# Routing attention and a gated feed-forward layer on one core: cluster masks through a TensorE product, weight conversion in two VectorE operations

## The chip, the cores and the metric

The kernel runs on one core of a Trainium2 chip. A core has five engines that run side by side and meet through semaphores: TensorE (PE in the profile) multiplies matrices into PSUM, VectorE (DVE), ScalarE (ACT) and GpSimd (POOL) work element by element, and SyncE (SP) issues transfers. The metric is the device time of one execution in microseconds (us). Before the change the median of four runs is 1229.87 us (1224.88 to 1232.32).

## The reference, cut to what matters

For each of 4 batches and 8 heads there are 768 queries and keys of 64 elements. Every query and every key is assigned to the nearest of 16 centroids of its head, and a query sees only the keys of its own cluster. The attention output, 3072 rows of 512, then goes through a feed-forward layer.

```python
q_assign = np.argmax(einsum(q_n, c_n), axis=-1)      # 16 clusters
k_assign = np.argmax(einsum(k_n, c_n), axis=-1)
mask = q_assign[:, :, :, None] == k_assign[:, :, None, :]
scores = np.where(mask, scale * q @ k.T, -1e9)
attn = softmax(scores);  x = attn @ v
h = x @ w_in                                          # 512 -> 2048
g = h * erf(softplus(h))
out = g @ w_out                                       # 2048 -> 512
```

The first maximum wins where two clusters tie, as argmax has it. The two weight matrices arrive as eight-byte floats, so they have to be made into four-byte ones on the chip.

## The kernel before, in words

**Attention.** The work goes by pairs of heads: 16 pairs, four to a batch. A pair has 12 units (two halves of the queries, six tiles of 128 keys). For a unit, `products` multiplies keys by queries in f32 and `scores` adds to it, in the same PSUM tile `sc`, a bf16 product `km` by `qm`. This second product carries the mask: `qm` holds, per query, ones at its cluster (and a row with its largest masked score), and `km` holds, per key, 0 at its own cluster and a hugely negative number at the others. One exponential on ScalarE makes `pr` from `sc`, GpSimd adds up `pr` into `acc`, and `attend` multiplies by the values into `av`. `divide` makes the reciprocal of the sums and writes `xT`, the input of the feed-forward layer.

**Preparing a pair.** What a pair needs beforehand is a generator, `aside(p)`, made of `route` and `shift` and cut into steps by its yields. `route` (line 272) has six steps: transpose the queries and keys; multiply them by the centroids into `psim`; transpose this into `sims`, take the maximum `mx` of each 16 and replace `sims` by a 0/1 comparison with it; copy the keys (`vectors("k")`); multiply by `rank` (16, 15, ... for queries, the same times 2 to the 60th for keys), take the maximum `mr` again, compare (queries: equal; keys: minus), giving `hot`, and transpose this to `hotT`; lastly spread `hotT` into `qm` and `km` by two VectorE and six ScalarE operations. The rank settles ties. `shift` (line 348) has fourteen steps: 24 bf16 products `sm` with a VectorE maximum `nmx` each, and for either half a transpose `pn`, a copy `nmT` on ScalarE and six small transfers that put the maxima into `qm`.

**Converting weights.** The weights come in 32 blocks (16 of `w_in`, 16 of `w_out`), each 128 x 512 eight-byte numbers, taken apart as the high word `hi` and the low word `lo`. `convert` (line 205) makes a block in three steps: the maximum with a tiny number of the magnitude that ScalarE has put into `x`; a shift by 3 and an AND of it, with the next transfer (`fetch`) issued behind; and an OR with two bits of `hi`, after which GpSimd adds the rounding summand `m` that ScalarE has made from `lo`. `split` holds the two ScalarE operations of the next block. `prepare(n)` runs n steps.

**The order of the work.** Through the first four pairs (48 slots, one per unit) nothing else is there to do, and every engine's order is the program's up to slot 44. A table `plan` says for each of a pair's 12 slots how many steps of its own `aside`, of the next pair's `aside` (before and after the scores) and of the conversion are run. From slot 45 on the feed-forward stream of `hidden` (products `hp`, copied to `g`), `gate` (softplus, erf, a product) and `project` (products `po`) is pumped between the attention's products, and a planner orders the instructions of each engine by its own costs. In that part `ASIDE` (line 45) lists the places at which a step of the next pair's `aside` is run, and the conversion is called with `prepare(2)` until it is done. `gate` and the last blocks of `w_out` share the tiles `a_s`.

PSUM has two buffers for `sc` and four (tag "x") for everything else: `psim`, `sm`, `pn`, `av`, `psum`, `hp`, `po`.

Of the kernel before, what the change touches and what calls it, by code (L numbers as in the profile page):

```python
# [8 lines left out]
F32 = mybir.dt.float32  # L9
BF16 = mybir.dt.bfloat16  # L10
U32 = mybir.dt.uint32
I32 = mybir.dt.int32
ALU = mybir.AluOpType
ACT = mybir.ActivationFunctionType
AX = mybir.AxisListType
# [17 lines left out]
LC = 512  # L33
TINY_HI = 2.0**-15
OUT_AT = (1, 2, 3, 4, 2, 3, 4, 2, 3, 4, 4, 3, 4, 4, 4, 4)
# [8 lines left out]

ASIDE = (*range(5), 6, *range(8, 8 + 2 * NJ), 10 + 2 * NJ, 12 + 2 * NJ)
REST = 3
# [20 lines left out]
def kernel(  # L67
# [36 lines left out]
    minus = const.tile([P, D], F32, name="minus")  # L104
    rank = const.tile([P, C], F32, name="rank")
    ccT = const.tile([P, HP, 2 * C], F32, name="ccT")
# [55 lines left out]
    for t in prs:  # L162
        ge.memset(t[:, :, HW : HW + 2], EPS)

# [31 lines left out]
    def split(n):  # L198

        if n < len(w_steps):  # L200
            hi, lo, m, x = steps[n]
            ae.activation(out=x.bitcast(F32), in_=hi.bitcast(F32), func=ACT.Abs)
            ae.activation(out=m.bitcast(I32), in_=lo, func=ACT.Copy, scale=2.0**-29)

    def convert():

        split(0)
        for n in range(len(w_steps)):
            hi, _, m, x = steps[n]
            w = w_steps[n][0]  # L210
            xf = x.bitcast(F32)
            ve.tensor_scalar(out=xf, in0=xf, scalar1=TINY_HI, scalar2=None, op0=ALU.max)
            yield
            ve.tensor_scalar(
                out=x, in0=x, scalar1=3, scalar2=0x3FFFFFFF,
                op0=ALU.logical_shift_left, op1=ALU.bitwise_and,
            )

            fetch(n - 2 if n < n_w_in else n - 1)
            yield  # L220
            ve.scalar_tensor_tensor(
                out=w.bitcast(U32), in0=hi, scalar=0xC0000000, in1=x,
                op0=ALU.bitwise_and, op1=ALU.bitwise_or,
            )

            ge.tensor_tensor(out=w.bitcast(I32), in0=w.bitcast(I32), in1=m.bitcast(I32), op=ALU.add)
            converted[0] = n + 1
            split(n + 1)
            yield
# [42 lines left out]
    def route(p):  # L272
# [20 lines left out]
        def vectors(nm):  # L293
# [12 lines left out]
        mx = routep.tile([P, n], F32, name="mx")  # L306
        ve.reduce_max(out=mx, in_=sim, axis=AX.X)
        ve.tensor_tensor(
            out=sim, in0=sim, in1=mx.unsqueeze(2).to_broadcast([P, n, C]), op=ALU.is_equal
        )  # L310
        yield
        vectors("k")
        yield

        ve.tensor_tensor(
            out=sim, in0=sim, in1=rank.unsqueeze(1).to_broadcast([P, n, C]), op=ALU.mult
        )
        mr = routep.tile([P, n], F32, name="mr")
        ve.reduce_max(out=mr, in_=sim, axis=AX.X)

        hot = routep.tile([P, HW], BF16, name="hot")
        for r, op in ((slice(0, D), ALU.is_equal), (slice(D, P), ALU.subtract)):
            ve.tensor_tensor(
                out=hot[r].rearrange("p (g c) -> p g c", c=C), in0=sim[r],
                in1=mr[r].unsqueeze(2).to_broadcast([D, n, C]), op=op,
            )
        hotT = routep.tile([P, HW], BF16, name="hotT")
        ve.transpose(out=hotT, in_=hot)
        yield
        late = []  # L330
        for half in range(2):
            cols = slice(half * HW, (half + 1) * HW)
            for e in range(2):
                r = slice(e * D, e * D + Q)
                g = slice(half * Q, (half + 1) * Q)
                if half == 0:
                    ve.tensor_scalar_mul(out=low["q"][r, e, cols], in0=hotT[g], scalar1=own[g, e : e + 1])
                else:
                    late.append((low["q"][r, e, cols], hotT[g], own[g, e : e + 1]))
                g = slice(D + half * Q, D + (half + 1) * Q)  # L340
                ae.copy(out=low["k"][r, e, cols], in_=hotT[g])
        for dst, src, scale in late:
            ae.activation(out=dst, in_=src, func=ACT.Copy, scale=scale)
        yield
# [245 lines left out]
    def prepare(n):  # L590
        for _ in range(n):
            next(conv, None)
# [3 lines left out]
    def aside(p):  # L596
# [5 lines left out]
    plan = (  # L602
        (1, 0, 1, 1), (1, 0, 2, 0), (1, 0, 2, 0), (1, 0, 1, 0), (0, 0, 0, 0), (0, 0, 2, 0),
        (0, 0, 2, 1), (0, 0, 2, 1), (0, 1, 0, 3), (0, 0, 0, 3), (0, 0, 2, 1), (0, 0, 1, 2),
    )
# [3 lines left out]
    def advance(p, n):  # L609
        for _ in range(n):  # L610
            next(ready[p])
# [11 lines left out]
    ve.memset(minus, -1.0)  # L623
    for c in range(C):
        ve.memset(rank[0:D, c : c + 1], float(C - c))
    ve.tensor_scalar_mul(out=rank[D:P], in0=rank[0:D], scalar1=BIG)
    ve.memset(alleps, S * EPS)
# [10 lines left out]
    products(1)  # L638
    advance(0, 4)
    prepare(2)  # L640
# [39 lines left out]
    for u in range(2 * NJ * HP, len(units), 2):  # L680
# [12 lines left out]
        for i in range(SLOTS):  # L693
# [3 lines left out]
            if not resting[0]:  # L697
                prepare(2)
            next(part, None)
# [41 lines left out]
```

## Time and profile before

| | |
|---|---|
| median of four runs | 1229.87 us |
| the profiled execution | 1224.88 us |
| its span, first to last instruction | 1223.1 us |
| PE busy | 1155.2 us, 94% of the span |
| DVE busy | 539.3 us, 44% |
| ACT busy | 568.1 us, 46% |
| POOL busy | 465.7 us, 38% |
| ACT table loads | 113 of 1283 ns |

The page gives the busy time of each engine, then the span cut into 40 slices of about 30.6 us with the busy share of each engine in tenths, the clock granted to PE, and the transfers. Other views group the instructions by operation and tile, follow the chain of work that ended last, or sum the busy time in stretches that one chooses. In a group's row the figures are: name of output and inputs, shapes, count, total busy us, mean ns of one, then the idle time of the engine before them and what ended it. All of the kernel's operations are issued through one helper, so that their rows carry its line, L58, and the names of the tiles tell them apart.

### The profile page before, as it was taken

What the parts mean: (1) busy time and instruction counts of PE and PEld (TensorE: products, weight loads), DVE (VectorE), ACT (ScalarE), POOL (GpSimd) and SP (SyncE); (2) the same over time, 40 slices, a digit from 0 to 9 for tenths busy, and PEclk for the clock granted to TensorE, in tenths of its full rate; (3) what the DMA queues carried; (4) which work ended last, traced back from release to release, by engine and by line L of the source; (5) the groups of instructions that cost most, each with busy time, mean ns of one, the idle gap of its engine ahead of it and who ended that gap; (6) DMA issues with size and microseconds to landing.
All of it is one profiled execution on the core that took longest, in us unless ns stands there. A gap on an engine that the chain in (4) does not pass through costs nothing.

```text
span 1223.1 us, 13359 instructions
## 1 busy us (share of the span) xinstructions
PE 1155.2 (94%) x4897; PEld 618.3 (51%) x4897; DVE 539.3 (44%) x999; ACT 568.1 (46%) x675; POOL 465.7 (38%) x462
## 2 busy tenths in 40 slices
PE   4888888889999999999999999999999999999998
PEld 1222235654454445465465455556456456576663
DVE  6899885674544335443353345344435112011121
ACT  3666656658342637175364454356263264132222
POOL 2467764446333344144243334235234343030200
PEclk7899999999999999999999999999999999999999
DMA  7444323122020202020110201002000000000000
GB/s 134 81 101 108 78 83 84 53 93 40 9 48 9 48 1 40 9 35 14 25 32 1 48 10 27 22 10 39 9 22 1 9 9 1 18 1 17 1 18 18
DMA packets 140753, 42.95 MB, mean 35 GB/s; under 512 B 133520, under 2 KB 133520, under 8 KB 140688
## 3 DMA queue, kind: packets, MB, share of 16 engines
q1 hardware_dynamic: 137552, 41.70, 15.1%
q10 hardware_dynamic: 3136, 0.39, 0.3%
q8 instruction: 39, 0.64, 0.2%
q14 instruction: 26, 0.21, 0.1%
HBM read 35.68 MB, written 6.29 MB: 34 GB/s over the span
## 4 chain that ended last, share of the span: by engine, by line
PE 74%; DVE 11%; issue 7%; ACT 6%; DMA 2%; POOL 1%; SPq 0%; ACTq 0%; DVEq 0%; POOLq 0%
PE po L58 25%; PE hp L58 24%; PE sc L58 12%; PE av L58 7%; PE sm L58 4%; DVE nmx L58 3%; ACT L58 2%; DVE w_out L58 2%; DVE den L58 1%; PE psum L58 1%; ACT inv L58 1%; DVE sims L58 1%; PE psim L58 1%; ACT km L58 1%; ACT a_s L58 1%
## 5 line engine op out<-in xcount | busy, mean ns | idle before, releaser
L58 PE MATMUL hp<-xT,w_in 128*128 128x256 f32 x1536 | 385.3, 388 | 3.3 <-DVE xT L58 2.4
L58 PE MATMUL po<-w_out,g 128*128 128x512 f32 x768 | 367.8, 597 | 0.6 <-DVE den L58 0.6
L58 POOL TENSOR_TENSOR acc<-acc,pr 128x384 f32<-128x384 f32 x256 | 240.1, 967 | 312.2 <-ACT pr L58 312.0
L58 PEld LDWEIGHTS hp<-xT,w_in 128*128 128x128 f32 x1536 | 287.8, 192 | 123.0 <-issue 79.2
L58 DVE TENSOR_REDUCE nmx<-sm 128x1 f32<-128x384 f32 x384 | 195.4, 551 | 140.4 <-PE sm L58 139.6
L58 ACT ACT_TABLE_LOAD x113 | 145.0, 1283 | 230.7 <-DVE g L58 128.8
L58 ACT ACTIVATE pr<-sc 128x768 f32<-128x768 f32 x192 | 147.4, 807 | 164.3 <-PE sc L58 164.0
L58 PEld LDWEIGHTS po<-w_out,g 128*128 128x128 f32 x768 | 141.8, 190 | 107.2 <-issue 94.4
L58 PE MATMUL sc<-qT,kT 64*128 64x384 f32 x768 | 182.5, 530 | 6.3 <-ACT pr L58 6.2
L58 POOL TENSOR_TENSOR g<-a_s,g 128x512 f32<-128x512 f32 x88 | 111.1, 1293 | 200.5 <-ACT a_s L58 200.5
L58 DVE COPY g<-hp 128x512 f32<-128x512 f32 x96 | 66.0, 687 | 256.5 <-PE hp L58 256.3
L58 PE MATMUL av<-pr,in_v 128*64 128x386 f32 x768 | 143.5, 502 | 2.9 <-DVE nmx L58 2.9
L58 PE MATMUL sm<-km,qm 128*128 128x384 bf16 x384 | 105.4, 340 | 29.9 <-DVE nmx L58 13.8
L58 PEld LDWEIGHTS sc<-qT,kT 64*128 64x128 f32 x768 | 70.4, 190 | 85.5 <-issue 44.3
L58 POOL TENSOR_TENSOR acc<-pr,pr 128x384 f32<-128x384 f32 x64 | 66.2, 1056 | 93.6 <-ACT pr L58 93.6
L58 PEld LDWEIGHTS av<-pr,in_v 128*64 128x64 f32 x768 | 49.8, 137 | 91.9 <-issue 77.3
L58 PEld LDWEIGHTS <-qm 128*128 128x128 bf16 x384 | 35.2, 99 | 97.0 <-issue 70.8
L58 DVE SCALAR_TENSOR_TENSOR den<-psum,inv 128x384 f32<-128x384 f32 x32 | 17.8, 558 | 145.5 <-ACT inv L58 145.0
L58 ACT ACTIVATE a_s<-a_s 128x2048 f32<-128x2048 f32 (+2 forms) x40 | 55.9, 1414 | 16.1 <-DMA a_s<-in_moe_w_out_dram 12.4
L58 ACT ACTIVATE a_s<-g 128x2048 f32<-128x2048 f32 x24 | 45.9, 1912 | 34.4 <-DVE g L58 33.0
L58 PE MATMUL sc<-qm,km 64*128 64x384 bf16 x384 | 58.7, 325 | 2.1 <-DMA qm<-nmT 2.1
L58 ACT COPY nmT<-pn 6x128 bf16<-6x128 bf16 x32 | 8.1, 252 | 95.2 <-PE pn L58 94.8
(66 smaller groups left out, 602.5 us busy)
## 6 DMA issues: line engine op xcount, KB each, us to landing
w_out<-in_moe_w_in_dram SPq DMA_DIRECT2D x16, 512.0 KB, 4.6
in_q<-in_q_dram SPq DMA_DIRECT2D x64, 96.0 KB, 3.2
in_v<-in_v_dram SPq DMA_DIRECT2D x32, 192.0 KB, 3.0
out_dram<-osb SPq DMA_DIRECT2D x24, 256.0 KB, 2.0
in_k<-in_k_dram SPq DMA_DIRECT2D x60, 96.0 KB, 3.4
a_s<-in_moe_w_out_dram SPq DMA_DIRECT2D x8, 512.0 KB, 3.7
w_out<-in_moe_w_out_dram SPq DMA_DIRECT2D x8, 512.0 KB, 4.2
qm<-nmT SPq DMA_DIRECT2D x192, 0.2 KB, 1.7
```

The source lines that it names most:

```text
L58: ins = getattr(self.engine, name)(*args, **kw)
```

## The change

**Masks.** After the comparison with `mx`, which now writes `hot` in bf16, the transpose to `hotT` follows at once; the product with `rank`, the second maximum `mr` and the two comparisons of 64 rows are gone. Instead a constant 128 x 128 bf16 matrix `first` is made at the start by GpSimd (one fill, three selections): within each block of 16 clusters it holds 1 on the diagonal and -1 for every earlier cluster. One bf16 product of `first` and `hotT` goes into a PSUM tile `won` (tag "x"), which is 1 where a cluster is the first maximum and 0 or less elsewhere. `qm` is made of it by a product with `own` and a maximum with 0 (VectorE, two operations) and by Relu with that scale (ScalarE, two operations); `km` by Identity with scale 2 to the 60th and bias minus that (ScalarE, four operations). These eight now read PSUM. `route` has five steps instead of six.

**Conversion.** A block takes two VectorE steps. ScalarE's Abs scales by 2 to the 16th, so that the maximum with 2.0 and a shift by 3 alone give the magnitude's bits. A new ScalarE operation in `signs` (Prelu) writes the sign into the upper 16 bits of each word of the summand `m`, and GpSimd's addition puts it in. The OR with `hi` is gone. `fetch` is called after the maximum, and the plan's conversion steps per pair go from 12 to 8, four blocks a pair as before.

**Order.** `plan` and `ASIDE` are rewritten for 19 instead of 20 steps; the conversion in the later part is called with 1 and 2 steps by turns.

```diff
-        ve.tensor_tensor(
-            out=sim, in0=sim, in1=mx.unsqueeze(2).to_broadcast([P, n, C]), op=ALU.is_equal
-        )
+        hot = routep.tile([P, HW], BF16, name="hot")
+        ve.tensor_tensor(
+            out=hot.rearrange("p (g c) -> p g c", c=C), in0=sim,
+            in1=mx.unsqueeze(2).to_broadcast([P, n, C]), op=ALU.is_equal,
+        )
+        hotT = routep.tile([P, HW], BF16, name="hotT")
+        ve.transpose(out=hotT, in_=hot)
         yield
         vectors("k")
         yield
-        ve.tensor_tensor(
-            out=sim, in0=sim, in1=rank.unsqueeze(1).to_broadcast([P, n, C]), op=ALU.mult
-        )
-        mr = routep.tile([P, n], F32, name="mr")
-        ve.reduce_max(out=mr, in_=sim, axis=AX.X)
-        hot = routep.tile([P, HW], BF16, name="hot")
-        for r, op in ((slice(0, D), ALU.is_equal), (slice(D, P), ALU.subtract)):
-            ve.tensor_tensor(
-                out=hot[r].rearrange("p (g c) -> p g c", c=C), in0=sim[r],
-                in1=mr[r].unsqueeze(2).to_broadcast([D, n, C]), op=op,
-            )
-        hotT = routep.tile([P, HW], BF16, name="hotT")
-        ve.transpose(out=hotT, in_=hot)
-        yield
+        won = ps_x.tile([P, HW], F32, name="won", tag="x")
+        te.matmul(won, lhsT=first, rhs=hotT, start=True, stop=True)
...
                 if half == 0:
-                    ve.tensor_scalar_mul(out=low["q"][r, e, cols], in0=hotT[g], scalar1=own[g, e : e + 1])
+                    ve.tensor_scalar(
+                        out=low["q"][r, e, cols], in0=won[g], scalar1=own[g, e : e + 1], scalar2=0.0,
+                        op0=ALU.mult, op1=ALU.max,
+                    )
                 else:
-                    late.append((low["q"][r, e, cols], hotT[g], own[g, e : e + 1]))
+                    ae.activation(
+                        out=low["q"][r, e, cols], in_=won[g], func=ACT.Relu, scale=own[g, e : e + 1]
+                    )
                 g = slice(D + half * Q, D + (half + 1) * Q)
-                ae.copy(out=low["k"][r, e, cols], in_=hotT[g])
-        for dst, src, scale in late:
-            ae.activation(out=dst, in_=src, func=ACT.Copy, scale=scale)
+                ae.activation(
+                    out=low["k"][r, e, cols], in_=won[g], func=ACT.Identity, bias=nbig[g], scale=BIG
+                )
...
-            ae.activation(out=x.bitcast(F32), in_=hi.bitcast(F32), func=ACT.Abs)
+            ae.activation(out=x.bitcast(F32), in_=hi.bitcast(F32), func=ACT.Abs, scale=UP)
...
+    def signs(n):
+        hi, _, m, _ = steps[n]
+        ae.activation(
+            out=m.bitcast(I16)[:, 1 : 2 * LC : 2], in_=hi.bitcast(F32), func=ACT.Prelu,
+            scale=2.0**-25, alpha=2.0**90,
+        )
...
-            ve.tensor_scalar(out=xf, in0=xf, scalar1=TINY_HI, scalar2=None, op0=ALU.max)
+            ve.tensor_scalar(out=xf, in0=xf, scalar1=2.0, scalar2=None, op0=ALU.max)
+            signs(n)
+            fetch(n - 2 if n < n_w_in else n - 1)
             yield
             ve.tensor_scalar(
-                out=x, in0=x, scalar1=3, scalar2=0x3FFFFFFF,
-                op0=ALU.logical_shift_left, op1=ALU.bitwise_and,
-            )
-            fetch(n - 2 if n < n_w_in else n - 1)
-            yield
-            ve.scalar_tensor_tensor(
-                out=w.bitcast(U32), in0=hi, scalar=0xC0000000, in1=x,
-                op0=ALU.bitwise_and, op1=ALU.bitwise_or,
+                out=w.bitcast(U32), in0=x, scalar1=3, scalar2=None, op0=ALU.logical_shift_left
             )
...
     plan = (
-        (1, 0, 1, 1), (1, 0, 2, 0), (1, 0, 2, 0), (1, 0, 1, 0), (0, 0, 0, 0), (0, 0, 2, 0),
-        (0, 0, 2, 1), (0, 0, 2, 1), (0, 1, 0, 3), (0, 0, 0, 3), (0, 0, 2, 1), (0, 0, 1, 2),
+        (1, 0, 1, 0), (1, 0, 2, 0), (1, 0, 1, 0), (1, 0, 0, 0), (0, 0, 1, 1), (0, 0, 1, 1),
+        (0, 0, 2, 1), (0, 0, 2, 1), (0, 1, 0, 2), (0, 1, 0, 0), (0, 0, 2, 1), (0, 0, 1, 1),
     )
...
-    advance(0, 4)
+    advance(0, 3)
...
-                prepare(2)
+                prepare(1 + i % 2)
```

## The prediction

> **What bounds the kernel now.** I read the page's line of 40 slices first, because an average over the span hides the stages.
>
> ```profile
> PE   4888888889999999999999999999999999999998
> DVE  6899885674544335443353345344435112011121
> PEclk7899999999999999999999999999999999999999
> ```
>
> From the tenth slice on (about 275 us) PE is full and VectorE half idle: there the time is PE's work. In the first nine PE is not full and VectorE nearly is. The change is about VectorE, so I cut that part by pairs of heads, each beginning with the transpose of its queries, and set the later part beside it (columns: busy us with counts for PE, weight loads, DVE, ACT, POOL; then the granted clock, the transfers' share and GB/s):
>
> ```profile
> 32.25:69.00 36.75, 31.18 (x152) 9.85 (x153) 30.51 (x57) 23.97 (x37) 20.03 (x20) 0.91 0.44 104
> 69.00:106.00 37.00, 31.63 (x166) 10.05 (x166) 33.85 (x61) 23.16 (x36) 25.55 (x25) 1.00 0.39 90
> 106.00:142.50 36.50, 31.19 (x156) 9.70 (x156) 31.79 (x59) 22.85 (x37) 24.06 (x24) 0.95 0.38 90
> 142.50:180.00 37.50, 28.99 (x143) 10.59 (x142) 33.01 (x54) 21.60 (x35) 28.26 (x25) 0.95 0.35 83
> 180.00:300.00 120.00, 109.05 (x493) 67.56 (x492) 74.88 (x129) 78.46 (x90) 65.12 (x57) 0.96 0.26 67
> 500.00:1223.00 723.00, 716.14 (x2921) 409.27 (x2919) 226.02 (x409) 290.35 (x306) 219.85 (x214) 1.00 0.07 17
> ```
>
> In the four pair periods VectorE has 31 to 34 of some 37 us, PE is idle for 5.57, 5.37, 5.31 and 8.51 us (24.8 together), and ScalarE has 13 to 16 us free per period. From 180 to 300 us PE is idle for another 11.0 us; after 500 us for 6.9 of 723. What can be won lies before 300 us.
>
> Then the chain that ended last, between 100 and 148 us (start, length, work): does it pass through the operations that go?
>
> ```profile
> 107.75 0.80 DVE w_out L58
> ...
> 112.74 1.10 DVE sims L58
> ...
> 113.86 0.56 DVE mr L58
> ...
> 114.45 0.55 DVE hot L58
> ...
> 115.01 0.57 DVE hot L58
> ...
> 134.98 0.69 DVE w_in L58
> ```
>
> It does: the product with the rank (1.10), the second maximum, both comparisons and an OR of the conversion stand on it. Their prices, before 300 us, are in the groups (count, total us, mean ns, idle before):
>
> ```profile
> L58 DVE SCALAR_TENSOR_TENSOR w_in<-w_out 128x512 uint32<-128x512 uint32 x16 | 13.2, 828 | 0.3
> L58 DVE TENSOR_TENSOR hot<-sims,mr 64x384 bf16<-64x384 f32 x14 | 10.7, 766 | 0.3
> L58 DVE TENSOR_TENSOR sims<-sims,rank 128x384 f32<-128x384 f32 x7 | 6.8, 973 | 0.1
> L58 DVE TENSOR_REDUCE mr<-sims 128x24 f32<-128x384 f32 x7 | 3.9, 551 | 0.2
> L58 ACT ACTIVATE w_out<-w_out 128x512 f32<-128x512 f32 x24 | 16.2, 674 | 18.4 <-DMA w_out<-in_moe_w_out_dram 12.9 <-DMA w_out<-in_moe_w_in_dram 5.3
> L58 ACT ACTIVATE qm<-hotT,own 32x384 bf16<-32x384 bf16 x12 | 7.4, 614 | 0.2
> ```
>
> **VectorE, per pair.** Away go 0.97 (rank), 0.55 (second maximum) and 2 x 0.77 (comparisons), 3.06 us; and four ORs at 0.83, 3.31 us. The comparison with the maximum stays (0.80 in this part; its bf16 output I cost at nothing, the row of the 64-row comparisons writes bf16 too). The shift loses its AND: its row has 724 ns, the maximum's 598; I take 724, so no gain, with 0.13 x 4 = 0.5 us as the other end. The two `qm` operations now read f32 in PSUM: today 611 ns from bf16; `den` from PSUM has 558. Taken 558, a gain of 0.1. Together 6.5 us of about 32.
>
> **ScalarE, per pair.** Four sign operations: the nearest row is Abs of the same size, 674 ns, so 2.7 us (0.58 from the 128x384 Ln with a pointer operand, 0.83 from the 64x768 copies as ends: 2.3 to 3.3). The `km` writes rise from 509 to about 582 (that Ln reads PSUM with a bias pointer), 0.3 us; the `qm` ones go from 614 to 582. ScalarE goes from 23 to 26 us: still free time, but whatever is queued behind the sign operation, an exponential as a rule, comes up to 0.7 us later. Up to 180 us that hides under the free 13 us and the two `sc` buffers; if the cover went, 4 x 2.7 = 11 us a side would show in the four pairs.
>
> **PE, per pair.** One `won` product. The nearest row, `sm`, has 340 ns alone, and the chain gives two of them 0.33 together: 0.16 to 0.34. PE meets it a step after the transpose, so it waits for nothing; VectorE's two `qm` operations now wait for PE, and behind them stand one conversion step and the next `nmx`, which need later products anyway. The first `sm` comes one slot after the spread instead of two; it needs only the first two `km` writes (1.2 us behind an exponential), and PE has 2.3 us of work in between. Taken: nothing more.
>
> **Other moves.** `first` is made on POOL, which stands idle for 20.8 us then; one fill and three selections at 0.2 and 0.3 us end long before 14 us. The rank's small fills on VectorE (0.4 us) lie beside the wait for `psim`. The first half's `pn` moves from slot 8 to slot 9; its six transfers take 3.7 us on SP and are needed at the next pair's slot 0, three slots or some 9 us on: hidden, else up to 3 us a pair. `fetch` comes half a block earlier on SP; it waits there for POOL's addition, and the maxima's transfers and the next pair's loads stand behind it. It was so before (three `w_out` issues took 4.0 us of SP at 95.6 us); nothing either way, a microsecond a pair as an end.
>
> **Start, up to 32 us.** Today `hotT` is done at 16.9, the masks at 20.3, Abs at 21.0, the maxima `nmx` begin at 21.9. Now `hotT` begins 2.35 us earlier, at 14.0, and ends at 14.6; `won` at 15.1; six ScalarE writes at 0.58 to 18.6; Abs 19.2; two conversion steps on VectorE; `nmx` at about 20.1. Gain 1.8 us, between 0 and 3.
>
> **The four pairs.** 6.5 us less VectorE work per pair can't all show, since PE's 31 us become the floor: at most its idle 5.3 to 8.5 us. I take 2.8 per pair, half of the usual 5.6, since some of that idle is the loop from `sm` over `nmx` to a free PSUM buffer: slots with four `sm` last 3.05 us for 2.4 us of PE work, three such remain of four (2 us), and the wait for `inv` and `den` stays. 4 x 2.8 = 11.2; ends 0 and 24.8.
>
> **180 to 300 us.** Sixteen sign operations, 10.8 us, fall where ScalarE has 78.5 of 120 us and the chain already runs through softplus, erf and table loads. Against that: 16 x 0.9 us of VectorE gone, and one block more done when the feed-forward begins. I take a gain of 2; ends 8 lost, 8 won.
>
> **After 300 us.** PE's work sets the time. Twelve `won` cost 1.9 to 4.1 us, and each holds one of four PSUM buffers while six ScalarE operations wait for their turn. Taken 4; ends 1.9 and 12.
>
> Sum: -1.8 - 11.2 - 2 + 4 = -11.0 against the profiled execution's 1224.88 (its span 1223.1 and 1.8 around it), so 1213.9. That execution is 5.0 under the median 1229.87, so I predict 1218.9, rounded to 1219.
>
> **Two rules of the skill.** The sign operation has 0.67 us on ScalarE by the row of Abs, and a single-source VectorE operation of that size 0.60 by the row of the maximum. The Trainium skill ("ScalarE: Activation LUTs", Rules for kernel authors) says relu and max belong on VectorE; costing each move by busy time alone, 16 signs in the pairs at 0.07 more would make the change 1.1 us worse. The windows say otherwise: ScalarE has free time there and VectorE hardly any. The `qm` operations lose a bf16 SBUF source, 611 ns, for PSUM, 558 by the nearest row. The skill ("VectorE: DVE Perf Modes", Why PSUM operands drop a tier) says that this costs a speed tier; that would add about 0.3 us a pair by an estimate from its table of modes, but today's row shows no fast tier to lose.
>
> **The rivals.** *PE nearly fills up.* All of VectorE's delay goes: 20 us of the 24.8, with 5 from 180 to 300: 1.8 + 20 + 5 - 4 = 23 less, 1207. For it: VectorE is on the chain at the removed operations. Against: waits of PE for `sm` buffers remain. *No gain.* The chain is only re-routed, over ScalarE and the `sm` loop: 1.8 + 2.2 - 4, 1230. For it: PE has 85% already, and its clock of 0.91 to 0.95 there isn't VectorE's doing. *Slower, by `won`'s buffer.* Late, `won` waits for ScalarE behind a gate's block; softplus, erf and three loads take 2 x 1.91 + 3 x 1.28 = 7.7 us, and the six readers 3.5 more. With `av`, `po` and `won` in three of four buffers, PE stops after one `hp` tile (3.5 us): up to 7.5 lost. If half of the twelve meet a gate, that is 45 us at worst, two thirds of it 30, and 1229.87 - 15 + 30 = 1245. It decides once the average loss of twelve passes 1.8 us, for then it eats the 15 us gained earlier and 6 more. For it: the chain between 199 and 242 us goes through ScalarE. Against: `pn` has the same form, read from PSUM by ScalarE 32 times, and PE idles only 6.9 us after 500.
>
> **How the numbers follow.** A measurement here can tell about 0.5%, 6.1 us, from no change: 1223.7 to 1236.0. Forecast 0.65 (its own range 1211 to 1225), PE full 0.12, no gain 0.12, slower 0.11. Faster: 0.62 + 0.12 = 0.74; same: 0.03 + 0.11 = 0.14; slower: 0.01 + 0.11 = 0.12. The range leaves out most of the slower rival and half of the fast one: 1205 to 1234.
>
> **What would show it.** Right: pair periods of about 34 us instead of 37, VectorE at 25 to 27 us in them, PE idle near 2.8; `nmx` first at 20 us; the late part longer by some 4 us; no more table loads than 113 or so. Wrong: pair periods unchanged with PE waiting for ScalarE or the transfers of `qm`; `won` rows followed by long PE idle; ScalarE full from 200 to 280 us with exponentials late; `hp` starting no sooner.

## The result, and the profile after

The changed kernel takes 1230.28 us (median of 43 runs), the kernel before beside it 1227.84 (64 runs): a ratio of 1.0022, with a 95% interval of 1.0012 to 1.0032. It is slower by some 2.7 us, which is inside the 0.5% that the prediction called no change. The forecast was 1219 and faster. The profiled execution of the changed kernel has a span of 1226.9 us against 1223.1, so the pair of profiles shows 3.8 us of loss to be explained. (In the changed kernel the helper's line is L60.)

The slices of the page:

```profile
PE   4888979799999989999999999999999999999998
DVE  5677864553443432333253244343425112011121
ACT  4687776687333545183364355255264254032222
PEclk8899989999999999999999999999999999999999
```

VectorE fell in the first nine slices, as meant, ScalarE rose there, and PE still has slices below full. Cut by pairs of heads, and the same later parts as before (columns as above: the stretch and its length, busy us of PE, weight loads, DVE, ACT, POOL, then clock and transfers):

```profile
32.25:70.40 38.15, 31.62 (x152) 9.96 (x152) 25.14 (x49) 26.59 (x42) 20.87 (x21) 0.87 0.47 116
70.40:104.70 34.30, 30.41 (x167) 9.93 (x163) 26.39 (x52) 25.84 (x41) 24.39 (x25) 1.00 0.41 97
104.70:139.20 34.50, 30.61 (x167) 9.85 (x163) 27.02 (x53) 26.01 (x41) 24.58 (x25) 1.00 0.38 83
180.00:300.00 120.00, 108.95 (x508) 66.65 (x507) 55.48 (x102) 87.83 (x102) 59.72 (x54) 1.00 0.24 60
500.00:1226.90 726.90, 716.52 (x2913) 408.40 (x2911) 209.19 (x380) 291.43 (x306) 219.50 (x214) 1.00 0.07 16
```

VectorE's work per pair is 25 to 27 us, from 31 to 34. But the first period is longer than before (38.2 us, from 36.8), and the next two are 34.3 and 34.5, from 37.0 and 36.5: VectorE is no longer what fills them, and PE is still idle for 3.9 to 6.5 us in each.

What took VectorE's place is read from the chain that ended last, here between 114 and 122 us:

```profile
114.45 0.28 PE won L60
...
114.76 0.62 DVE qm L60
...
115.40 0.58 ACT km L60
...
116.01 0.62 DVE qm L60
...
116.65 0.57 ACT km L60
...
117.25 0.57 ACT qm L60
...
118.44 0.57 ACT qm L60
...
119.62 0.68 ACT w_out L60
...
120.33 1.10 DVE w_out L60
121.43 0.48 DVE nmx L60
...
121.95 0.32 PE sm L60
```

One can follow it downwards. The product `won` is made; VectorE writes a part of `qm`; only then does ScalarE write a part of `km`, only then VectorE its second part, and so on: the two engines take turns at `won`. Behind the six ScalarE writes stands an Abs of the conversion (the row `ACT w_out`), behind it VectorE's maximum (`DVE w_out`), behind that in VectorE's queue the `nmx`, and PE's next `sm` waits for the buffer that `nmx` frees. Before the change the same place on the chain was VectorE's own work.

The prices of the new operations, before 300 us (count, total us, mean ns, idle before and what ended it; the `w_in` row is the shift of the 16 blocks of `w_in`):

```profile
L60 ACT ACTIVATE w_out<-w_out 128x512 int16<-128x512 f32 x24 | 18.7, 779 | 0.3
L60 ACT ACTIVATE km<-won,nbig 32x384 bf16<-32x384 f32 x28 | 16.1, 574 | 11.8 <-DVE qm L60 11.5
L60 DVE TENSOR_SCALAR qm<-won,own 32x384 bf16<-32x384 f32 x14 | 8.5, 606 | 13.9 <-PE won L60 9.4 <-ACT km L60 4.5
L60 DVE TENSOR_SCALAR w_in<-w_out 128x512 uint32<-128x512 uint32 x16 | 6.7, 420 | 0.2
L60 PE MATMUL won<-hotT,first 128*128 128x384 bf16 x7 | 2.3, 335 | 0.5 <-DVE hotT L60 0.5
```

The idle columns matter here: VectorE stood still for 13.9 us in front of 14 `qm` writes, and ScalarE for 11.8 in front of 28 `km` writes.

**A clock for the later part.** Every chunk of the feed-forward layer has two softplus operations (`a_s<-g`), 24 in all, and each comes at the same point of that layer's work in both kernels. Their starts give how far one kernel is ahead of the other:

| softplus | before, us | after, us | after minus before |
|---|---|---|---|
| 1st | 200.38 | 194.22 | -6.2 |
| 5th | 412.80 | 405.95 | -6.9 |
| 6th | 465.52 | 459.68 | -5.8 |
| 9th | 616.63 | 615.94 | -0.7 |
| 15th | 903.04 | 906.68 | +3.6 |
| 24th | 1193.92 | 1197.72 | +3.8 |

So the change is 6 to 7 us ahead at 200 us and again at 412, and then loses 10.7 to the end, 9.6 of them between the sixth and the last softplus. In between, at the second to fourth, the lead reads 4.3, 14.9 and 10.1 us: there the planner sets how the two layers' work is mixed, and a lead is not yet time won. Two questions follow: why 6 and not the 13 that I had summed up for the start and the pairs, and what loses 10.7 later.

### The profile page after: what moved, and what is told of

The parts are those of the page before. It is cut to its first block, busy times and chain, and to the rows that moved or that the text cites. A ratio compares the mean times of both kernels' runs of the same rounds, so it can differ in the third digit from the quotient of the medians.

```text
span 1226.9 us, 13280 instructions
## 1 busy us (share of the span) xinstructions
PE 1160.2 (95%) x4913; PEld 620.0 (51%) x4913; DVE 472.2 (38%) x887; ACT 589.2 (48%) x705; POOL 461.1 (38%) x466
## 4 chain that ended last, share of the span: by engine, by line
PE 73%; ACT 10%; DVE 8%; issue 7%; DMA 2%; POOL 1%; ACTq 0%; SPq 0%; DVEq 0%; POOLq 0%
PE po L60 25%; PE hp L60 23%; PE sc L60 13%; PE av L60 6%; PE sm L60 4%; ACT a_s L60 2%; ACT L60 2%; ACT km L60 2%; DVE nmx L60 2%; DVE den L60 1%; PE psim L60 1%; ACT inv L60 1%; DVE w_out L60 1%; ACT qm L60 1%; ACT pr L60 1%
## 5 line engine op out<-in xcount | busy, mean ns | idle before, releaser
L60 PE MATMUL hp<-xT,w_in 128*128 128x256 f32 x1536 | 385.4, 387 | 6.3 <-DVE xT L60 4.6
L60 PE MATMUL po<-w_out,g 128*128 128x512 f32 x768 | 368.6, 598 | 0.6 <-DVE den L60 0.6
L60 POOL TENSOR_TENSOR acc<-acc,pr 128x384 f32<-128x384 f32 x256 | 239.5, 965 | 313.0 <-ACT pr L60 313.0
L60 PEld LDWEIGHTS hp<-xT,w_in 128*128 128x128 f32 x1536 | 286.8, 192 | 128.8 <-issue 81.4
L60 DVE TENSOR_REDUCE nmx<-sm 128x1 f32<-128x384 f32 x384 | 195.7, 550 | 134.9 <-PE sm L60 133.9
L60 ACT ACTIVATE pr<-sc 128x768 f32<-128x768 f32 x192 | 148.0, 806 | 164.9 <-PE sc L60 164.4
L60 PEld LDWEIGHTS po<-w_out,g 128*128 128x128 f32 x768 | 141.8, 190 | 106.5 <-issue 93.6
L60 PE MATMUL sc<-qT,kT 64*128 64x384 f32 x768 | 186.8, 533 | 3.7 <-ACT pr L60 3.6
L60 POOL TENSOR_TENSOR g<-a_s,g 128x512 f32<-128x512 f32 x88 | 109.9, 1279 | 201.9 <-ACT a_s L60 201.9
L60 DVE COPY g<-hp 128x512 f32<-128x512 f32 x96 | 66.0, 687 | 280.8 <-PE hp L60 280.7
L60 PE MATMUL av<-pr,in_v 128*64 128x386 f32 x768 | 141.9, 499 | 0.8 <-DVE nmx L60 0.8
L60 PE MATMUL sm<-km,qm 128*128 128x384 bf16 x384 | 106.5, 342 | 33.8 <-DVE nmx L60 15.4
L60 PEld LDWEIGHTS sc<-qT,kT 64*128 64x128 f32 x768 | 71.7, 190 | 83.4 <-issue 46.5
L60 POOL TENSOR_TENSOR acc<-pr,pr 128x384 f32<-128x384 f32 x64 | 64.3, 1026 | 104.3 <-ACT pr L60 104.3
L60 PEld LDWEIGHTS av<-pr,in_v 128*64 128x64 f32 x768 | 49.5, 137 | 89.9 <-issue 76.9
L60 PEld LDWEIGHTS <-qm 128*128 128x128 bf16 x384 | 35.4, 99 | 97.6 <-issue 86.1
L60 DVE SCALAR_TENSOR_TENSOR den<-psum,inv 128x384 f32<-128x384 f32 x32 | 17.8, 556 | 141.6 <-ACT inv L60 141.2
L60 ACT ACTIVATE a_s<-a_s 128x2048 f32<-128x2048 f32 (+3 forms) x48 | 62.0, 1308 | 12.4 <-DMA a_s<-in_moe_w_out_dram 11.9
L60 PE MATMUL sc<-qm,km 64*128 64x384 bf16 x384 | 60.5, 327 | 2.7 <-DMA qm<-nmT 2.7
L60 ACT ACTIVATE a_s<-g 128x2048 f32<-128x2048 f32 x24 | 45.9, 1912 | 34.4 <-DVE g L60 34.0
L60 ACT ACTIVATE km<-won,nbig 32x384 bf16<-32x384 f32 x64 | 36.7, 574 | 36.0 <-DVE qm L60 35.3
```

The costliest lines, as they stand in the source:

```text
L60: ins = getattr(self.engine, name)(*args, **kw)
```

## The experiments

Theory L: the masks are dear, by the product, its PSUM buffer and its readers on two engines, and late above all. Theory C: the conversion's sign operations, 32 more on ScalarE, ate the gain. All ratios are to the kernel before on the same chip, with their 95% intervals; the changed kernel's is 1.0022. A run's profile is a single execution, and early times in it scatter: runs 8 and 12, which are one kernel, have the first softplus at 185.2 and 183.2 us, and the first pair period is 36.7 to 38.1 us in the changed kernel and runs 6, 9 and 10, which do not differ up to its end. The stretch from the sixth softplus to the last is steadier: 726.7 us in both of runs 8 and 12, and 738.0 in the changed kernel and in runs 1 and 7, which make the later masks in the same way. The code blocks show the lines that matter; ... stands for the rest.

### 1. The new masks alone

```diff
-            signs(n)
...
-                out=w.bitcast(U32), in0=x, scalar1=3, scalar2=None, op0=ALU.logical_shift_left
+            ve.scalar_tensor_tensor(
+                out=w.bitcast(U32), in0=hi, scalar=0xC0000000, in1=x,
...
-        (1, 0, 1, 0), (1, 0, 2, 0), (1, 0, 1, 0), (1, 0, 0, 0), (0, 0, 1, 1), (0, 0, 1, 1),
-        (0, 0, 2, 1), (0, 0, 2, 1), (0, 1, 0, 2), (0, 1, 0, 0), (0, 0, 2, 1), (0, 0, 1, 1),
+        (1, 0, 1, 0), (1, 0, 2, 0), (1, 0, 1, 0), (1, 0, 0, 0), (0, 0, 1, 2), (0, 0, 1, 1),
+        (0, 0, 2, 1), (0, 0, 2, 1), (0, 1, 0, 3), (0, 1, 0, 0), (0, 0, 2, 2), (0, 0, 1, 2),
```

> The new masks alone; the conversion is that of before, its 12 steps per pair laid over the new plan. Theory L (the masks cost late: a product, a PSUM buffer, readers on two engines, about 10 us lost after 412 us where before and after trade places) expects 3 to 8 us slower than before (1231 to 1236), the first softplus 2 to 4 us earlier than before's 200 us. Theory C (the conversion's sign operations on ScalarE ate the gain) expects 4 to 8 us faster than before (1220 to 1224).

Measured: 1235.9 us, ratio 1.0070 (1.0047 to 1.0093): slower than before. Theory L's number, and its late loss (738.0 us from the sixth softplus to the last); but the first softplus comes at 200.65 us, level with the kernel before and not 2 to 4 us ahead. The profiled execution, at 1242.1 us, is the slowest of the six.

### 2. The new conversion alone

```diff
+            signs(n)
...
-            ve.scalar_tensor_tensor(
-                out=w.bitcast(U32), in0=hi, scalar=0xC0000000, in1=x,
-                op0=ALU.bitwise_and, op1=ALU.bitwise_or,
+                out=w.bitcast(U32), in0=x, scalar1=3, scalar2=None, op0=ALU.logical_shift_left
```

> The new conversion alone; route and the first three columns of the plan are those of before. Theory L expects 3 to 7 us faster than before (1221 to 1225), with nothing lost after 412 us. Theory C expects 0 to 4 us slower than before (1228 to 1232).

Measured: 1214.5 us, ratio 0.9891 (0.9865 to 0.9918), better than either theory had it. Theory C has fallen: with all the sign operations in place the first softplus comes at 188.1 us, pair periods are 34.8, 34.4 and 34.6, and from the sixth softplus to the last it takes 728.4 us, as long as before. The conversion alone gives the pairs as much as the whole change does; beside it the masks take another 3 us of VectorE work off each pair and, as the plan has them, give nothing there. The parts do not add: by the ratios, 13.4 less and 8.6 more would make 4.8 less, and together they are 2.7 more.

### 3. Without the product

```diff
-        won = ps_x.tile([P, HW], F32, name="won", tag="x")
-        te.matmul(won, lhsT=first, rhs=hotT, start=True, stop=True)
+        won = hotT
```

> The changed kernel without the product won: the eight writes read hotT in SBUF, so ties between clusters are no longer settled. Theory L expects the late loss gone: 6 to 10 us faster than the changed kernel (1220 to 1224), the eight writes side by side on two engines as in the kernel before. Theory C expects at most 3 us, from the product's own 16 x 0.33 us on PE.

Measured: 1219.2 us, ratio 0.9932 (0.9908 to 0.9956), 11 us faster than the changed kernel. The pair periods are 35.2, 33.0 and 33.2. It speaks for theory L, but takes away product, PSUM and turns at once (and leaves ties between clusters unsettled). VectorE still waits 9.8 us for an Abs in six times between 32 and 140 us, so the Abs is not all that held the pairs: gone are its waits for `won`, 5.5 us in the changed kernel. The stretch from the sixth softplus to the last is 740.9 us, longer than with the product, in an execution that was the slowest of the six; what made it longer is told behind run 14. In the profile the gain was made early.

### 4. The product copied to SBUF

```diff
+        wonb = routep.tile([P, HW], BF16, name="wonb")
+        ve.tensor_copy(out=wonb, in_=won)
+        won = wonb
```

> The changed kernel with one VectorE copy of won from PSUM to bf16 in SBUF (16 x 0.55 us more on VectorE) and the eight writes reading that. If the two engines' turns at the PSUM tile (0.64 and 0.68 us of waiting between km and qm writes, 4.8 us for all eight) are what costs, 3 to 7 us faster than the changed kernel (1223 to 1227). If the product itself and the order that the planner makes of it cost, within 2 us of it (1228 to 1232).

Measured: 1223.0 us, ratio 0.9968 (0.9946 to 0.9990), 7 us faster than the changed kernel, although VectorE does 16 copies more. Reading SBUF, the two engines write side by side, and VectorE's own `qm` writes take half the time (0.31 us in the median, 0.61 from PSUM), which pays for the copy of 0.56. Of the 7 us, the profile (an execution of 1225.4) shows 1.6 us of lead at 412 us and little later (737.4 us from sixth to last). Its second and third pair periods are 34.3 and 34.5 us, no shorter, but at a granted clock of 0.95 where the changed kernel had 1.00; run 5, with the changed kernel's first pairs at 0.95, has 34.9 and 35.3.

### 5. New masks in the first four pairs only

```diff
-ASIDE = (*range(5), *range(8, 8 + 2 * NJ), 10 + 2 * NJ, 12 + 2 * NJ)
+ASIDE = (*range(5), 6, *range(8, 8 + 2 * NJ), 10 + 2 * NJ, 12 + 2 * NJ)
...
+        if p >= HP:
+            yield from old_masks(p, st, low, sim, mx, n, vectors)
+            return
```

> The changed kernel, but only the first four pairs make their masks by the product; the later twelve make them as before (rank, second maximum, copies from SBUF, 20 steps). Theory L, that the masks are dear late, expects the profile's lead of 7 us before 412 us to stay to the end: 1218 to 1223, 7 to 12 us faster than the changed kernel. If the masks cost in the first four pairs only, 1228 to 1232.

Measured: 1218.6 us, ratio 0.9919 (0.9893 to 0.9946). The lead at the fifth softplus is the changed kernel's (405.99 us against 405.95), and from the sixth to the last it takes 727.0 us, where the changed kernel takes 738.0. That the late loss is the late masks' is shown by this run, with their place in the order counted among them, since the old `ASIDE` is back as well.

### 6. Late masks on VectorE alone

```diff
-                if half == 0:
+                if half == 0 or p >= HP:
...
+                if p >= HP:
+                    ve.tensor_scalar(
+                        out=low["k"][r, e, cols], in0=won[g], scalar1=BIG, scalar2=-BIG,
+                        op0=ALU.mult, op1=ALU.add,
+                    )
+                    continue
```

> The changed kernel, but the later twelve pairs write all eight masks on VectorE, from won in PSUM: the product stays, ScalarE's six late writes and the two engines' turns go. If the late loss comes from ScalarE's writes standing in front of the logarithm that divide waits for, 5 to 9 us faster than the changed kernel (1221 to 1226). If it comes from the product and its PSUM buffer, within 2 us of it (1228 to 1233).

Measured: 1223.3 us, ratio 0.9972 (0.9952 to 0.9991), 6 us faster than the changed kernel with the product and its buffer still there; 732.2 us from the sixth softplus to the last. More than half of the late loss hangs on ScalarE as a writer.

The trace of the changed kernel shows how. Two late stretches, of ScalarE (start, us) and of PE:

```profile
550.76 0.57 ACT L60 ACTIVATE qm<-won,own 32x384 bf16<-32x384 f32 x1
551.35 0.58 ACT L60 ACTIVATE km<-won,nbig 32x384 bf16<-32x384 f32 x1
551.93 0.57 ACT L60 ACTIVATE qm<-won,own 32x384 bf16<-32x384 f32 x1
552.52 0.57 ACT L60 ACTIVATE km<-won,nbig 32x384 bf16<-32x384 f32 x1
553.11 1.28 ACT L60 ACT_TABLE_LOAD   x1
554.41 0.58 ACT L60 ACTIVATE inv<-psum,alleps 128x384 f32<-128x384 f32 x1
```

```profile
559.55 0.70 PE L60 MATMUL hp<-xT,w_in 128*128 128x256 f32 x2 [1.06 <-DVE xT L60]
```

The mask writes stand in front of the logarithm `inv` that `divide` begins with. `den` and `xT` come behind it, and PE's next `hp` needs `xT`. The same place in the kernel before:

```profile
551.21 0.51 ACT L58 COPY km<-hotT 32x384 bf16<-32x384 bf16 x1 [0.31 <-DVE hotT L58]
556.25 0.58 ACT L58 ACTIVATE inv<-psum,alleps 128x384 f32<-128x384 f32 x1
556.86 0.51 ACT L58 COPY km<-hotT 32x384 bf16<-32x384 bf16 x1
561.99 0.59 PE L58 MATMUL hp<-xT,w_in 128*128 128x256 f32 x2
```

One `km` copy stands in front of the logarithm, one behind it, the other writes behind the exponential, and PE does not wait.

### 7. No conversion step behind the masks

```diff
-        (1, 0, 1, 0), (1, 0, 2, 0), (1, 0, 1, 0), (1, 0, 0, 0), (0, 0, 1, 1), (0, 0, 1, 1),
-        (0, 0, 2, 1), (0, 0, 2, 1), (0, 1, 0, 2), (0, 1, 0, 0), (0, 0, 2, 1), (0, 0, 1, 1),
+        (1, 0, 1, 0), (1, 0, 2, 0), (1, 0, 1, 0), (1, 0, 0, 1), (0, 0, 1, 0), (0, 0, 1, 0),
+        (0, 0, 2, 1), (0, 0, 2, 1), (0, 1, 0, 2), (0, 1, 0, 1), (0, 0, 2, 1), (0, 0, 1, 1),
```

> The changed kernel with the plan's conversion steps of slots 4 and 5 moved to slots 3 and 9. In the changed kernel VectorE's maximum in slot 5 waits 2.1 us for an Abs behind six mask writes on ScalarE, and PE 1.8 us behind it. If that wait holds the pairs back, pair periods of 32.5 to 33.5 us instead of 34.4 and 1223 to 1227. If not, periods of 34 or more and 1228 to 1232.

Measured: 1222.0 us, ratio 0.9954 (0.9934 to 0.9974), 8 us faster than the changed kernel for two numbers moved in a table. The transposes that open the pairs start at

```profile
32.19 0.97 DVE L60 STREAM_TRANSPOSE qT<-in_q 128x768 f32<-128x768 f32 x1
66.80 0.96 DVE L60 STREAM_TRANSPOSE qT<-in_q 128x768 f32<-128x768 f32 x1
99.66 0.96 DVE L60 STREAM_TRANSPOSE qT<-in_q 128x768 f32<-128x768 f32 x1
132.70 0.96 DVE L60 STREAM_TRANSPOSE qT<-in_q 128x768 f32<-128x768 f32 x1
```

which makes periods of 34.6, 32.9 and 33.0 us, against 38.1, 34.3 and 34.5. The waits between 32 and 140 us (us in total, times, longest), two of the changed kernel and one of this run:

```profile
DVE w_out L60 <- ACT w_out L60: 9.6, 5, 2.1
PE sm L60 <- DVE nmx L60: 6.1, 5, 1.8
PE sm L60 <- DVE nmx L60: 3.1, 10, 0.7
```

Of the waits of VectorE for an Abs only one of 1.0 us, at a block in an `a_s` tile, is left there in this run, and PE waits 3.1 us for `nmx` instead of 6.1. The wait was named beforehand and the second and third period are as expected from its removal, so that the chain through ScalarE held the pairs is shown; run 3 shows a second way to shorten the same chain. Late it loses as the changed kernel does (738.0).

### 8. The three costs taken away, masks early only

```diff
(edits of 4, 5 and 7 together)
```

> New masks in the first four pairs only, won copied to SBUF by VectorE, and the two conversion steps moved as in the run before: each of the three supposed costs taken away. If they are the costs and add up, 1210 to 1216, as fast as the new conversion alone (1214.5) or faster. If the masks bring nothing even so, 1216 to 1222.

Measured: 1210.2 us, ratio 0.9849 (0.9826 to 0.9873); run once more below. The pair periods are 35.1, 32.3 and 32.5, the last two 0.6 us shorter than in run 7 at the same clock of 1.00: that is what the copy is worth to a pair. From the sixth softplus to the last it takes 726.7 us.

### 9. No product in the later pairs

```diff
+        if p >= HP:
+            won = hotT
+        else:
             won = ps_x.tile([P, HW], F32, name="won", tag="x")
             te.matmul(won, lhsT=first, rhs=hotT, start=True, stop=True)
```

> The changed kernel, but the later twelve pairs read hotT in SBUF instead of the product won, on the same two engines and in the same places; late ties are no longer settled. If the product and its PSUM buffer make the late loss, 6 to 10 us faster than the changed kernel (1219 to 1223). If the place of the mask writes in the order makes it (ahead of the logarithm that divide waits for), at most 3 us faster, 1226 to 1231, with PE still waiting for xT.

Measured: 1229.2 us, ratio 1.0022 (1.0002 to 1.0041), the changed kernel's own ratio. Taking the late product away brings nothing while the writes stay where they are: from the sixth softplus to the last it takes 741.1 us, and in this trace PE still waits for `xT`, 2.1 us in two times between 412 and 1000 us, and 3.3 us for `den`.

### 10. The late masks behind the start of divide

```diff
-ASIDE = (*range(5), *range(8, 8 + 2 * NJ), 10 + 2 * NJ, 12 + 2 * NJ)
+ASIDE = (*range(4), 6, *range(8, 8 + 2 * NJ), 10 + 2 * NJ, 12 + 2 * NJ)
```

> The changed kernel with one number of ASIDE altered: the late step that writes the masks is run at place 6, as the last step of route was before, instead of place 4, and so comes behind the start of divide. If the place makes the late loss, 5 to 10 us faster than the changed kernel (1219 to 1224) and the waits of PE for xT gone. If the product and its buffer make it, within 2 us of it (1227 to 1232).

Measured: 1224.4 us, ratio 0.9988 (0.9970 to 1.0005), 4 us faster than the changed kernel. ScalarE at the same place of the work:

```profile
547.91 0.58 ACT L60 ACTIVATE inv<-psum,alleps 128x384 f32<-128x384 f32 x1
...
553.98 0.57 ACT L60 ACTIVATE km<-won,nbig 32x384 bf16<-32x384 f32 x1 [2.24 <-DVE qm L60]
555.23 0.57 ACT L60 ACTIVATE km<-won,nbig 32x384 bf16<-32x384 f32 x1 [0.68 <-DVE qm L60]
```

and what PE then meets:

```profile
555.85 0.32 PE L60 MATMUL sm<-km,qm 128*128 128x384 bf16 x1 [0.93 <-ACT km L60]
```

The logarithm is in front now and the waits for `xT` are gone, but the writes, still in turns, come close to the `sm` that need them: PE waits 4.5 us for `km` between 412 and 1000 us. One wait became another, and only 1.6 us of the stretch from sixth to last are won (736.4), which is one stretch of lowered clock fewer (behind run 14).

### 11. All three, in all sixteen pairs

```diff
(edits of 4, 7 and 10 together)
```

> New masks in all sixteen pairs with won copied to SBUF, the two conversion steps moved to slots 3 and 9, and the late mask writes at place 6. If place, turns and the step behind the masks are all that made the new masks dear, 1208 to 1214, level with new masks in the first four pairs alone. If the product itself costs late, 3 to 6 us more than that, 1213 to 1219.

Measured: 1212.6 us, ratio 0.9881 (0.9859 to 0.9904), 732.8 us from sixth to last. Taking the turns away as well wins 3.6 us late. The time lies in the first expected band (1208 to 1214) and just under the second. Beside run 12, made on the same chip, it is 4.8 us slower, which is the second's 3 to 6, though the two intervals overlap.

### 12. The eighth version again

```diff
(the kernel of 8, unchanged)
```

> The version with new masks in the first four pairs only, won copied and the steps moved, once more on this chip beside the one before it: 1208 to 1214.

Measured beside it: 1207.8 us, just under the band, ratio 0.9860 (0.9835 to 0.9885). New masks in the first four pairs only remain the better choice, and both runs of this version beat the conversion alone (0.9891) by 3 to 4 thousandths, though the intervals overlap.

### 13. All three, late masks without the product

```diff
(the kernel of 11, with `won = hotT` for p >= HP)
```

> The version with all three costs taken away in all sixteen pairs (1212.6), but its later twelve pairs read hotT in SBUF and make no product and no copy; late ties are no longer settled. If what is left of the late loss is the product (nine of 0.33 us after 412 us), 2 to 5 us faster, 1207 to 1211, level with new masks in the first four pairs alone. If it is the place of the writes on two engines still, 1212 to 1216.

Measured: 1213.1 us, ratio 0.9898 (0.9882 to 0.9915): no faster than with the product, so the first expectation was wrong. In its trace the planner puts other work between the logarithm and its follower, VectorE does `den` late again, and PE waits for `xT`, 2.3 us in two times.

### 14. A late product that nobody reads

```diff
         ve.transpose(out=hotT, in_=hot)
         yield
+        won = ps_x.tile([P, HW], F32, name="won", tag="x")
+        te.matmul(won, lhsT=first, rhs=hotT, start=True, stop=True)
         late = []
```

> The version with new masks in the first four pairs only (1207.8 to 1210.2), with the product won made in the later twelve pairs too and read by nobody: the masks there are still those of before. If a late product costs its own time on PE, 12 x 0.17 to 12 x 0.34, 2 to 5 us slower. If a product hides, within 1 us. Should it cost 8 us or more, the late loss was the product's after all.

Measured: 1217.4 us, ratio 0.9928 (0.9907 to 0.9948), against 0.9849 and 0.9860 without it: 8 to 10 us, past both small answers and in the third, though runs 9 and 13 say that leaving the late product out does not end the loss. From the sixth softplus to the last it takes 729.4 us, 2.7 more than without: about the product's own time there, seven at 0.33. Another 4 to 5 us are lost between the first softplus and the sixth, where the product waits 2.3 us in two times for a PSUM buffer behind `den`, and PE's waits for `nmx` and `xT` are longer than in run 12 (4.9 and 2.1 us, from 1.6 and 0.2). So an added product is not cheap either, and its price is not its duration.

**The granted clock in the later part.** One thing is in none of the theories. Between the sixth softplus and the last, PE's granted clock is full in every trace but for a few stretches of 3.4 us (in runs 3, 4 and 9 one of 6.8) in which it is half. The same two stretches of 10 us in the kernel before and in the changed one (two lines each; the clock is the third figure from the end):

```profile
560.00:570.00 10.00, 10.00 (x40) 5.19 (x39) 5.40 (x11) 4.37 (x7) 6.30 (x7) 1.00 0.00 0
740.00:750.00 10.00, 8.40 (x32) 5.09 (x31) 2.74 (x6) 5.91 (x8) 4.71 (x6) 0.83 0.24 38
560.00:570.00 10.00, 10.00 (x32) 4.43 (x31) 3.41 (x8) 1.51 (x2) 4.39 (x6) 0.83 0.00 0
740.00:750.00 10.00, 8.40 (x31) 5.01 (x31) 2.84 (x6) 6.59 (x9) 5.43 (x6) 0.83 0.16 25
```

A mean of 0.83 over 10 us is 1.7 us of PE's time lost. The kernel before loses it once there, the changed one twice, and the stretch that it has beyond the other's begins some 1.6 us after the wait for `xT` that ends at 559.55. Every such stretch in these traces begins within 2 us of a wait of PE of 0.89 us or more, but not every such wait is followed by one (none follows that of 0.89 us at 728 us in run 12), and no run separates the two. Taking the lost time off gives an estimate of what each stretch from sixth to last would be at full clock:

| kernel | sixth to last, us | lost to the clock, us | without it, us |
|---|---|---|---|
| before; run 2 | 728.4 | 1.7 | 726.7 |
| runs 5; 8 and 12 | 727.0; 726.7 | 0 | 727.0; 726.7 |
| run 14 (product, unused) | 729.4 | 0 | 729.4 |
| run 6 (all on VectorE) | 732.2 | 1.7 | 730.5 |
| run 11 (copied, place 6) | 732.8 | 1.7 | 731.1 |
| run 13 (no product, place 6) | 737.2 | 5.1 | 732.1 |
| run 4 (copied) | 737.4 | 5.1 | 732.3 |
| runs 3; 9 (no product) | 740.9; 741.1 | 6.8 | 734.1; 734.2 |
| changed; runs 1 and 7 | 738.0 | 3.4 | 734.6 |
| run 10 (place 6) | 736.4 | 1.7 | 734.7 |

Read so, the late masks cost 7.9 us as they are. Leaving out the product or moving the writes takes at most 0.5 of that away by itself; copying takes 2.3, copying and moving 3.5, writing on VectorE alone 4.1. What a kernel loses before the sixth softplus is not in this table: run 11 takes 59.7 us from the fifth to the sixth, at a clock of 0.89, where the kernel before takes 52.7 at 0.97.

**What stays open.** The late loss is the late masks' (run 5). ScalarE's writes in front of the logarithm are one part of it (6), the place and the turns together another cut through the same loss (10 and 11), and the lowered clock, which follows waits, a third. But the pieces do not add up: without the product the loss stays (9 and 13), and a product alone costs (14). Each edit makes the planner order the engines anew, and a wait of one or two microseconds moves from `xT` to `sm` or to a buffer. A clean price for each piece in this part cannot be given from these runs, and why a wait is sometimes followed by half the clock is not shown.

## Why the prediction was wrong

**The reading of the stages was right, and so was the sum of VectorE's work.** I had 25 to 27 us per pair, and it is 25.1, 26.4 and 27.0. The removed operations did stand on the chain, and the change ahead of 200 us does win time. Of single prices, the sign operation has 0.78 us (predicted 0.67), the shift alone 0.42 for `w_in` and 0.54 to 0.64 for `w_out` (0.72 taken, with a gain as the other end), while the maximum rose from 0.60 to 0.83, `qm` on VectorE 0.61 (0.56), `km` 0.57 (0.58). None of this decides anything.

**The step on PE per pair failed.** It said that "VectorE's two `qm` operations now wait for PE, and behind them stand one conversion step and the next `nmx`, which need later products anyway", and took nothing. The runs show a chain in its place: `won`, then eight writes of which the first four go in turns, an Abs, a maximum, `nmx`, `sm`, with 9.6 us of VectorE's waits for the Abs and 6.1 of PE's for `nmx` in three pairs. I had looked at what is queued behind the waiting VectorE operation, and not at what is queued behind the six ScalarE writes, a conversion's Abs for which VectorE then waits with `nmx` behind it. Run 7, which moves that step and the one behind it out of the way, has the 33 us periods.

**The start failed for a related reason.** I had 1.8 us by six ScalarE writes back to back while VectorE wrote its two. They took turns: the first `qm` write begins at 15.57 us, the last `km` write ends at 20.40, 4.8 us where the kernel before needs 3.4. `nmx` begins at 21.93, as before (21.86).

**The four pairs** should have given 2.8 each; the three whole periods gave 4.2 together (from 32.25 to 143.37, now 32.30 to 139.18), the first of them a loss of 0.9, at a clock of 0.87 against 0.91. The fourth stretch that I counted, 142.5 to 180 us, is no whole period: the next `qT` transpose comes at 200.49. With start and pairs I had 13.0 us by the time of the first softplus, and 6.2 came.

**180 to 300 us** was sized at a gain of 2; between the first and the fifth softplus the lead grows by 0.7. The feared loss of 8 did not come: run 2 carries the same sign operations without harm.

**After 300 us** I took 4 and gave 12 as the end; from the fifth softplus on it is 10.7. The mechanism that I priced, `won` holding a PSUM buffer while ScalarE works through a gate, is not what the trace shows. PE waits for `xT`, because the writes were put in front of `divide`'s logarithm. Of the 9.6 us between the sixth softplus and the last, 3.5 are more idle time of PE (2.1 for `xT`, 1.2 of `sm` for a buffer that the late `den` frees), 2.3 are the seven products there, and 1.7 the second stretch at half clock; some 2 us are not located. I had listed `ASIDE` as part of the change and not asked what stands at the place that it drops: route's last step moved from place 6 to place 4, in front of the start of `divide` in the program.

**The rivals.** The outcome is the number of the no-gain rival (1230), which had 0.12. Its reason, the chain re-routed over ScalarE, is right for the pairs; but a gain is there, and is given back late, by a loss that this rival has at 4. That the number was met is chance. Adding the terms as measured, 6.2 and 0.7 won and 10.7 lost, gives the 3.8 us between the two spans.

**The two rules of the skill.** The Trainium skill's advice to keep relu-like work off ScalarE ("ScalarE: Activation LUTs", Rules for kernel authors) would have refused the sign operation. Run 2 shows the exchange paying, with 0.78 us on an engine that had time. For `qm` from PSUM I set the row's 611 ns against "VectorE: DVE Perf Modes" (Why PSUM operands drop a tier) and saw no fast tier to lose. That was a misreading: 611 is a mean over writes that take from 306 to 1230 ns in that trace. The same write takes 310 ns in the median from the bf16 SBUF tile of run 4 and 604 to 609 each time from PSUM, so the traces agree with the section, at 0.6 us a pair for the two writes.

## What to carry to other kernels

When an operation's source moves from SBUF to a PSUM tile that two engines read, cost the readers one after the other, and copy the tile once if they matter: here a copy more on VectorE was 7 us cheaper, and it made the reads of that tile on VectorE half as long. For each operation that a change adds to a busy queue, name the next operation on that queue and who waits for it, on every engine that the change writes from, not only on the one that it relieves. When two traces differ by a few microseconds, compare the granted clock in the same stretch before looking for a cause in the order of the work. And do one half of a two-part change alone before judging it: here one half gave 1.1%, the other took 0.7%, and with the masks in the first four pairs, copied, and two steps moved, the sum is 1.4 to 1.5%.

## What the runs showed of the hardware that was not expected

Reads of one PSUM tile by VectorE and ScalarE were put in turns, with 0.64 and 0.68 us of idle time before the next reader, about one write each, though they read different partitions (0 to 31 and 64 to 95). VectorE's second `qm` write waits so once in each of the sixteen pairs (11.5 us together); the same writes from an SBUF tile started in the same moment (both at 545.17 us in run 11). The waits end on semaphores, and no run here shows what the engines would do without them.

A ScalarE operation on 128 x 512 elements took 0.67 us with a four-byte result and 0.78 with a two-byte one written to every other half-word. An estimate by the formula of the Trainium skill ("ScalarE: Activation LUTs", What ACT_TABLE_LOAD costs), which it gives for activations with immediate scale and bias, is 0.61 at that width. Both rows here are above it, the strided two-byte one more so; source and result are strided in that row, so that the width of the result alone does it is not shown.

After some waits of PE of 0.89 us or more its granted clock was half for 3.4 us, at 561 us in the changed kernel for instance, which makes such a wait cost 1.7 us more than it lasts.
